# A new order of work for a spectral gate, with the stores spread over the last stage and a new place for some small products

## Chip, cores, metric

One core of a Trainium2 chip. The metric is the device time of one execution in microseconds. The profiled span is 1.8 us shorter than that time, but 2.1 to 2.2 us shorter in the three kernels that have the small products on VectorE (`b_small_dve`, `a_small_dve`, `b_both`), so about 0.4 us of what these seem to gain in a profile is lost outside the span; why is not shown. Where two profiles are compared, spans are used, where two kernels are compared, times. A run is called slow here when it is over 1.5% above the fastest of the same kernel. Comparisons use fast runs.

## The reference

```python
def branch(x, w_r, w_i):                       # x: 1 x 2048 x 1024, bf16
    X = rfft2(x.astype(float32), axes=(-2, -1))
    return irfft2(X * (w_r + 1j * w_i), s=(2048, 1024)).astype(bfloat16)

g = sigmoid((A_x * gate_w).sum(-1, keepdims=True))
return g * branch(A_x, A_w_r, A_w_i) + (1 - g) * branch(A_x, B_w_r, B_w_i)
```

Both branches share the input, so there is one forward transform, then two products with weights, two inverse transforms and a mix.

## The kernel before

The transforms are matmuls on TensorE. ScalarE and VectorE move the results out of PSUM, VectorE does folds, products and sums. The kernel is a list of named tasks. Each task names its engine and buffers, and each engine does its tasks in the order of the list; semaphores are derived from what the tasks read and write.

```python
SUMS = {(0, 3): 1, (0, 5): 1, (1, 6): 1}   # units (branch, j) summed on VectorE before the inverse transform
ORDER = """
mz:g x12:s F:s table:a warm:p0 x14:s x2:s x0:s x8:s x4:s w0.0.0.1:s fold6.0.2:d0 ...
... i1.15:p2 evv1.10:a p1.6.0:d2 i1.14:p1 evv1.15:a
gzg:d v5.1:p3 ps1.6.1:d evv1.14:a i1.11:p0 ...
... out10:s q12a:d s1i15:p00 y0b:d4 evo14.0:a out4:s evo14.1:a y12b:d1 out2:s q14a:d out0:s ...
"""
# name:engine+buffers; p TensorE, a ScalarE, d VectorE, g GpSimd, s the DMA queue
names = {"p": "pe", "a": "act", "d": "dve", "g": "pool", "s": "sp"}
```

The names that matter: `w1.*` load the second branch's weights; `p1.j.t` are its products and `ps1.j.t` their sums (VectorE); `i1.T` is the first inverse transform of row T (32 matmuls, or 16 if the unit is summed), `evv1.T` its eviction; `dinv`, `evd` the second inverse transform and its eviction; `s1i`, `evo` the mix of both branches; `q`, `h`, `y` the last sums, `out` a store of 512 or 256 KB. `p5.b` are the products of the single column l = 512, `v5.b` the 24 small matmuls that need them, `vf.b` the copy of that column into the row of all others:

```python
def e_p5(e_, b=b):           # four operations on 16 or 32 elements per partition
    x = ap(X5, 0, [[16, 2], [1, 16]]); r = ["X5"] + wk[b]        # X5 and all weights of the branch
    S.op("pool", [tt(ap(P5, o, ...), x, ap(T_, 512, ...), ALU.mult)], r, [("p5", b, 0)])
    S.op("pool", [tt(ap(P5, o + 32, ...), x, ap(T_, NS + 512, ...), ALU.mult)], r, [("p5", b, 1)])
    for c, op in enumerate((ALU.subtract, ALU.add)):
        S.op("pool", [tt(..., op)], [("p5", b, c)], [("P5", b, c)])
# the store of a group: one DMA, issued when both halves of its sums are there
S.op("sp", [lambda e: e.dma_start(outv[:, n:n + nn, :], yy(yb, 0, [[1, 1024]]))],
     [("y", yb.i, 0), ("y", yb.i, 1)], [], dma="out")
```

Of the kernel before, what the change touches and what calls it, by code (L numbers as in the profile page):

```python
# [13 lines left out]
SUMS = {(0, 3): 1, (0, 5): 1, (1, 6): 1}  # L14
# [7 lines left out]
mz:g x12:s F:s table:a warm:p0 x14:s x2:s x0:s x8:s x4:s w0.0.0.1:s fold6.0.2:d0 fold6.1.2:d1 fold6.0.1:d0  # L22
fold6.0.0:d0 fold6.1.1:d1 fold6.1.0:d1 neg2:a neg3:d DM:s fod6.1.1:d fod6.1.0:d fod6.0.1:d neg0:a fod6.0.0:d
w0.0.0.0:s s1.6.1:p1 neg1:a fold7.0.2:d0 fold7.0.1:d0 fold7.1.2:d1 fold7.1.0:d1 s1.6.0:p2 GW:s evz6.1:a fold7.1.1:d1
fold7.0.0:d0 SK:s fod7.1.1:d fod7.1.0:d s1.7.1:p3 fold1.0.0:d3 fold1.1.2:d2 fold1.0.1:d3 fold1.1.1:d2 evz6.0:a
fod7.0.0:d fod7.0.1:d w0.0.1.0:s fold1.1.0:d2 fold1.0.2:d3 s1.7.0:p0 fod1.1.0:d fod1.1.1:d evz7.1:a fold0.1.2:d2
fold0.0.0:d3 fold0.0.1:d3 fold0.0.2:d3 fold0.1.1:d2 fod0.0.0:d s1.1.1:p1 fod0.0.1:d evz7.0:a fod1.0.0:d fold0.1.0:d2
s1.0.0:p2 fod1.0.1:d fold4.0.0:d5 fold4.0.1:d5 fold4.1.2:d4 fod0.1.1:d fod0.1.0:d fold4.1.0:d4 s1.1.0:p3 evz0.0:a
fold4.1.1:d4 s1.0.1:p0 fold4.0.2:d5 fod4.1.0:d fod4.1.1:d evz1.1:a s1.5.1:p2 fold2.1.2:d1 fold2.0.1:d0 fold2.0.0:d0
# [341 lines left out]
def build(nc, A_x, A_w_r, A_w_i, B_w_r, B_w_i, gate_w, out):  # L371
# [53 lines left out]
    def tt(o, a, b, op):  # L425
        return lambda e: e.tensor_tensor(out=o, in0=a, in1=b, op=op)  # L426
# [673 lines left out]
```

## Time and profile before

| | before |
|---|---|
| time, median of 3 (range) | 125.28 us (125.12 to 125.44) |
| profiled span | 123.70 us |
| last sum over | 119.04 us |
| span behind the last sum | 4.66 us |
| TensorE's wait for the small products | 1.3 us |

How to read it: TensorE, VectorE and ScalarE are each busy for 86 to 91% of the span, so no engine can be called the bound; one has to ask, stage by stage, what the next stage waits for.

### The profile page before, as it was taken

The page shows a single profiled execution, that of the slowest core. Times are in us where ns is not written, and L with a number is a line of the kernel's source. Part 1 is how long each engine was busy: PE and PEld are TensorE (multiplying, and loading weights), DVE is VectorE, ACT ScalarE, POOL GpSimd, SP SyncE. Part 2 cuts the span into 40 slices and gives each one's busy share as a digit, 9 for nine tenths or more (in the row PEclk, how much of TensorE's full clock was granted, in tenths as well). Part 3 has the DMA queues.
Part 4 walks back from the last instruction along what each step waited for, and adds up shares of the span by engine and source line. Part 5 has one row for each costly group of instructions (what it writes and reads, how often), then busy time and mean ns, then how long its engine had stood idle before and what let it go on. Part 6 is the DMA issues. An engine that isn't in the chain of part 4 may idle for free.

```text
span 123.7 us, 4183 instructions
## 1 busy us (share of the span) xinstructions
PE 112.6 (91%) x1853; PEld 84.8 (69%) x1853; DVE 108.4 (88%) x155; ACT 105.8 (86%) x119; POOL 14.6 (12%) x22
## 2 busy tenths in 40 slices
PE   5999999999999999999999995999999999999700
PEld 2377888855768755886898895999967656476300
DVE  0589899699999999999999997699879989999940
ACT  4187799699999999997999999789988999999700
POOL 2000000220000069000000498000000000000000
PEclk9999999999999999999999999999999999999996
DMA  4999999677785878685027000000000000170897
GB/s 86 409 440 424 303 215 206 187 210 203 223 235 168 218 204 260 172 215 184 0 52 209 16 0 5 5 1 0 5 0 0 0 5 0 42 297 0 339 409 269
DMA packets 13425, 19.23 MB, mean 155 GB/s; under 512 B 2656, under 2 KB 10848, under 8 KB 13152
## 3 DMA queue, kind: packets, MB, share of 16 engines
q1 hardware_dynamic: 13408, 18.98, 49.0%
q8 instruction: 14, 0.23, 0.8%
q14 instruction: 3, 0.02, 0.1%
HBM read 14.77 MB, written 4.19 MB: 153 GB/s over the span
## 4 chain that ended last, share of the span: by engine, by line
PE 56%; ACT 25%; POOL 6%; SPq 3%; DMA 3%; issue 1%; DVE 1%; ACTq 0%; DVEq 0%; POOLq 0%
PE PS L423 56%; ACT R L430 17%; ACT RING L430 8%; POOL P L426 6%; SPq L446 3%; DMA R<-in_B_w_i_dram 3%; POOL R L516 0%; ACTq L287 0%; DVE RING L426 0%; DVEq L287 0%; DVE R L426 0%; POOLq L287 0%; ACT X L430 0%; POOLq L1085 0%
## 5 line engine op out<-in xcount | busy, mean ns | idle before, releaser
L430 ACT ACTIVATE R<-PS 128x1024 bf16<-128x1024 f32 (+1 forms) x97 | 90.1, 1079 | 6.6 <-PE PS L423 6.4
L426 DVE TENSOR_TENSOR RING<-R 128x2048 bf16<-128x2048 bf16 (+2 forms) x69 | 58.1, 897 | 5.4 <-DMA R<-in_A_x_dram 5.3
L423 PE MATMUL PS<-DM,R 128*128 128x128 bf16 (+1 forms) x384 | 34.2, 246 | 0.0
L423 PEld LDWEIGHTS PS<-DM,R 128*128 128x128 bf16 x384 | 28.8, 98 | 4.8 <-ACT R L430 0.4
L423 PE MATMUL PS<-SK,RING 64*128 64x128 bf16 x928 | 28.9, 217 | 1.0 <-ACT R L430 0.8
L423 PEld LDWEIGHTS PS<-SK,RING 64*128 64x128 bf16 x928 | 26.5, 103 | 4.3 <-ACT R L430 2.6
L431 DVE CAST R<-PS 128x1024 bf16<-128x1024 f32 x17 | 20.4, 1221 | 3.1 <-PE PS L423 3.0
L423 PE MATMUL PS<-R,FM 128*128 128x512 bf16 (+1 forms) x80 | 17.7, 358 | 0.0
L426 DVE TENSOR_TENSOR R<-R 128x512 bf16<-128x512 bf16 (+2 forms) x30 | 13.8, 512 | 0.5 <-ACT R L430 0.3
L426 POOL TENSOR_TENSOR P<-X,R 128x32 bf16<-128x32 bf16 x4 | 9.2, 2330 | 38.7 <-DMA R<-in_B_w_i_dram 20.2
L423 PEld LDWEIGHTS PS<-R,FM 128*128 128x128 bf16 x80 | 7.4, 98 | 6.8 <-ACT R L430 1.3
L430 ACT ACTIVATE RING<-PS 128x1024 bf16<-128x1024 f32 x11 | 10.7, 1060 | 0.5 <-PE PS L423 0.5
L423 PE MATMUL PS<-FM,RING 128*128 128x256 bf16 (+1 forms) x74 | 9.3, 281 | 0.0
L423 PE MATMUL PS<-RING,SK 64*64 64x512 bf16 (+1 forms) x128 | 8.9, 384 | 0.3 <-ACT R L430 0.2
L423 PEld LDWEIGHTS PS<-FM,RING 128*128 128x128 bf16 x74 | 7.2, 98 | 1.9 <-DVE RING L426 0.2
L423 PE MATMUL PS<-R 128*128 128x512 bf16 x16 | 5.8, 542 | 1.3 <-POOL R L516 1.3
L423 PE MATMUL PS<-FM,R 128*128 128x256 bf16 x56 | 6.8, 273 | 0.0
L431 DVE CAST RING<-PS 128x1024 bf16<-128x1024 f32 x5 | 6.1, 1223 | 0.3 <-PE PS L423 0.2
L423 PEld LDWEIGHTS PS<-FM,R 128*128 128x128 bf16 x56 | 5.4, 98 | 0.9 <-DVE R L426 0.3
L423 PEld LDWEIGHTS PS<-RING,SK 64*64 64x64 bf16 x128 | 2.7, 105 | 4.6 <-ACT RING L430 1.7
L423 PEld LDWEIGHTS PS<-R 128*128 128x128 bf16 x16 | 2.0, 133 | 4.5 <-issue 2.7
L426 DVE TENSOR_TENSOR R<-RING 128x512 bf16<-128x512 bf16 (+1 forms) x10 | 4.8, 527 | 0.0
(38 smaller groups left out, 36.3 us busy)
## 6 DMA issues: line engine op xcount, KB each, us to landing
out_dram<-RING SPq DMA_DIRECT2D x7, 512.0 KB, 3.6
R<-in_A_x_dram SPq DMA_DIRECT2D x4, 512.0 KB, 5.9
R<-in_A_x_dram SPq DMA_DIRECT2D x2, 1024.0 KB, 10.2
R<-in_A_w_r_dram SPq DMA_DIRECT2D x15, 128.2 KB, 3.1
R<-in_A_w_i_dram SPq DMA_DIRECT2D x15, 128.2 KB, 3.0
R<-in_B_w_r_dram SPq DMA_DIRECT2D x15, 128.2 KB, 3.0
R<-in_B_w_i_dram SPq DMA_DIRECT2D x15, 128.2 KB, 3.1
FM<-c_F SPq DMA_DIRECT2D x1, 512.0 KB, 4.6
```

The lines of the kernel that those rows point to most:

```text
L423: return lambda e: e.matmul(o, l, r, start=start, stop=stop, skip_group_check=True)
L426: return lambda e: e.tensor_tensor(out=o, in0=a, in1=b, op=op)
L430: return lambda e: e.activation(o, i, ACT.Copy)
L431: return lambda e: e.tensor_copy(o, i)
L446: t.emit = lambda g: S.op(eng, [lambda e, d=d, s=s: e.dma_start(d, s, **kw) for d, s in pairs], reads, writes, dma=kind, after=after)
```

## The change

Its words: a new order of work, the stores spread over the last stage, and the small products of l = 512 of the second branch on VectorE. The diff, without most of the list of tasks:

```diff
-SUMS = {(0, 3): 1, (0, 5): 1, (1, 6): 1}
+SUMS = {(0, 1): 1, (0, 4): 1, (1, 3): 1, (1, 7): 1}
 ORDER = """
-mz:g x12:s F:s ... w1.4.1.0:s ... RM:s ... w1.8.1.1:s w1.12.0.0:s ... w1.12.0.1:s ... GS:s ... w1.12.1.0:s
+mz:g x2:s F:s ... w1.12.0.0:s ... grow:p0 RM:s ... w1.8.1.1:s ... vf0:s ... w1.12.0.1:s ... w1.12.1.0:s
-... ps1.4.0:d p5.1:g i1.7:p3 ... i1.14:p1 evv1.15:a gzg:d v5.1:p3 ps1.6.1:d ...
+... dinv0.9:p2 evd0.8:a p5.1:g dinv0.3:p3 ps1.3.0:d ... i1.13:p1 ps1.7.0:d v5.1:p3 ...
-... out6 ... out8 ... out10 ... out4 ... out2 ... out0 ... out12 ... out14 ... out15
+... out2 ... out4 ... out10 ... out8 ... out6 ... out0 ... out12 ... out15 ... out14
 """
-        p5 = add(f"p5.{b}", due("v", 1 + b), {"pool": (5.0, 5.2)}, None, ...)
+        p5 = add(f"p5.{b}", due("v", 1 + b), {"pool": (7.5, 7.7), "dve": (0.6, 0.7)}, None, ...)
-            S.op("pool", [tt(ap(P5, o, ...
+            S.op(e_, [tt(ap(P5, o, ...            # likewise in the other three operations
+        o.bytes, o.tail = nn * 262144 / 410e3, 0.3   # estimates for the ordering, not used on the chip
```

More of the change, by code (lines that the diff above doesn't have):

```diff
@@ L21 @@
 ORDER = """
-mz:g x12:s F:s table:a warm:p0 x14:s x2:s x0:s x8:s x4:s w0.0.0.1:s fold6.0.2:d0 fold6.1.2:d1 fold6.0.1:d0
-fold6.0.0:d0 fold6.1.1:d1 fold6.1.0:d1 neg2:a neg3:d DM:s fod6.1.1:d fod6.1.0:d fod6.0.1:d neg0:a fod6.0.0:d
-w0.0.0.0:s s1.6.1:p1 neg1:a fold7.0.2:d0 fold7.0.1:d0 fold7.1.2:d1 fold7.1.0:d1 s1.6.0:p2 GW:s evz6.1:a fold7.1.1:d1
-fold7.0.0:d0 SK:s fod7.1.1:d fod7.1.0:d s1.7.1:p3 fold1.0.0:d3 fold1.1.2:d2 fold1.0.1:d3 fold1.1.1:d2 evz6.0:a
-fod7.0.0:d fod7.0.1:d w0.0.1.0:s fold1.1.0:d2 fold1.0.2:d3 s1.7.0:p0 fod1.1.0:d fod1.1.1:d evz7.1:a fold0.1.2:d2
@@ L27 @@
-fold0.0.0:d3 fold0.0.1:d3 fold0.0.2:d3 fold0.1.1:d2 fod0.0.0:d s1.1.1:p1 fod0.0.1:d evz7.0:a fod1.0.0:d fold0.1.0:d2
-s1.0.0:p2 fod1.0.1:d fold4.0.0:d5 fold4.0.1:d5 fold4.1.2:d4 fod0.1.1:d fod0.1.0:d fold4.1.0:d4 s1.1.0:p3 evz0.0:a
-fold4.1.1:d4 s1.0.1:p0 fold4.0.2:d5 fod4.1.0:d fod4.1.1:d evz1.1:a s1.5.1:p2 fold2.1.2:d1 fold2.0.1:d0 fold2.0.0:d0
-fold2.1.1:d1 evz0.1:a s1.4.1:p1 fold2.1.0:d1 evz1.0:a fod4.0.1:d fod2.1.1:d fod2.1.0:d s1.2.1:p0 fod4.0.0:d evz5.1:a
-s1.3.1:p3 fold2.0.2:d0 evz4.1:a s1.5.0:p2 evz3.1:a w0.0.1.1:s fod2.0.0:d s1.4.0:p1 fod2.0.1:d evz2.1:a s1.2.0:p3
@@ L32 @@
-evz4.0:d w0.4.0.0:s evz5.0:a s1.3.0:p0 evz2.0:d d0.1:p10 evz3.0:a d2.1:p21 d3.1:p31 d3.0:p31 gj:p0 d2.0:p21 evq3:a
-g8:d d0.0:p10 evq2:d g9:g d10.1:p02 w0.4.0.1:s d10.0:p02 evq0:a d11.0:p32 d11.1:p32 qc1:d d1.0:p20 evq10:a evq11:d
-d1.1:p20 w0.4.1.0:s s2.1.1:p1 evq1:a s2.1.0:p0 evx1.1:d s2.5.0:p3 w0.4.1.1:s evx1.0:a s2.0.0:p2 qc0:d qc5:d s2.0.1:p1
-evx0.0:d evx5.0:a w0.8.0.0:s d14.0:p01 d14.1:p01 evx0.1:a p0.1.0:d0 s2.5.1:p3 d15.0:p21 w0.8.0.1:s evx5.1:a d15.1:p21
-evq14:d d5.1:p10 ps0.1.0:d evq15:a d5.0:p10 d4.1:p30 w0.8.1.0:s p0.1.1:d0 d6.0:p02 evq5:a d4.0:p30 d6.1:p02 d7.1:p22
@@ L37 @@
-qc7:d evq4:a w0.8.1.1:s evq6:d ps0.1.1:d d7.0:p22 s2.7.1:p1 evq7:a s2.2.0:p3 qc2:d evx7.1:d w0.12.0.0:s s2.7.0:p0
-evx2.0:a s2.2.1:p2 p0.0.1:d1 d9.0:p11 evx2.1:a d9.1:p11 w0.12.0.1:s i0.3:p3 p0.0.0:d1 evq9:a ps0.0.1:d i0.2:p2
-w0.12.1.0:s evx7.0:a evv0.3:d ps0.0.0:d d8.1:p11 evv0.2:a w0.12.1.1:s d8.0:p11 p0.5.1:d0 d12.0:p00 d13.1:p30 evq8:a
-d13.0:p30 d12.1:p00 p0.5.0:d0 w1.0.0.0:s evq13:a s2.4.0:p2 s2.4.1:p1 evq12:d evx4.0:a i0.0:p3 w1.0.0.1:s evx4.1:a
-qc3:d ps0.5.0:d i0.1:p2 qc6:d evv0.0:a qc4:d ps0.5.1:d w1.0.1.0:s x5:p0 s2.6.0:p1 p0.2.1:d1 x5e:a evv0.1:a s2.6.1:p3
@@ L42 @@
-p5.0:g w1.0.1.1:s i0.11:p0 p0.2.0:d1 evx6.0:a ps0.2.1:d i0.10:p2 evv0.11:a p0.4.0:d0 w1.4.0.0:s ps0.2.0:d i0.4:p1
-evx6.1:a i0.5:p0 p0.4.1:d0 ps0.4.0:d w1.4.0.1:s evv0.4:a s2.3.0:p3 p0.6.1:d1 ps0.4.1:d evv0.5:a s2.3.1:p1 w1.4.1.0:s
-p0.6.0:d1 evx3.1:a ps0.6.1:d i0.9:p0 RM:s evx3.0:a p0.7.1:d2 i0.8:p1 ps0.6.0:d evv0.10:a i0.13:p3 p0.7.0:d2 w1.8.0.0:s
-ps0.7.1:d evv0.9:a v5.0:p2 p0.3.0:d0 ps0.7.0:d v5e.0:a w1.8.0.1:s i0.14:p0 evv0.13:a p0.3.1:d0 i0.12:p2 w1.4.1.1:s
-evv0.14:a ps0.3.0:d grow:p3 evv0.8:a p1.0.1:d1 w1.8.1.1:s evv0.12:a ps0.3.1:d i0.15:p0 ps1.0.1:d p1.0.0:d1 w1.12.0.0:s
@@ L47 @@
-i0.7:p1 evv0.15:a p1.1.0:d2 ps1.0.0:d i1.1:p2 w1.8.1.0:s evv0.7:a i0.6:p0 p1.1.1:d2 ps1.1.0:d DI:s i1.0:p1 evv0.6:a
-p1.2.1:d0 ps1.1.1:d evv1.0:a vf0:s i1.3:p0 w1.12.1.1:s p1.2.0:d0 evv1.1:a ps1.2.1:d i1.2:p1 evv1.3:a p1.3.0:d1
-w1.12.0.1:s ps1.2.0:d i1.4:p2 evv1.2:a gzr:d GS:s ps1.3.0:d i1.5:p0 w1.12.1.0:s evv1.4:a p1.4.1:d2 dinv0.3:p1 evv1.5:a
-p1.3.1:d1 dinv0.7:p3 ps1.4.1:d evd0.3:a dinv0.11:p2 p1.4.0:d2 ps1.3.1:d dinv0.9:p0 evd0.7:a i1.6:p1 p1.5.1:d0 evd0.9:a
-ps1.4.0:d p5.1:g i1.7:p3 evd0.11:a p1.5.0:d0 ps1.5.1:d gzt:p0 evv1.6:a p1.7.0:d1 i1.9:p2 ps1.5.0:d evv1.7:a i1.8:p1
@@ L52 @@
-p1.7.1:d1 ps1.7.0:d evv1.9:a i1.10:p3 p1.6.1:d2 evv1.8:a ps1.7.1:d i1.15:p2 evv1.10:a p1.6.0:d2 i1.14:p1 evv1.15:a
-gzg:d v5.1:p3 ps1.6.1:d evv1.14:a i1.11:p0 ps1.6.0:d v5e.1:a i1.13:p2 evv1.11:d i1.12:p1 evv1.13:a gmix1:p3 evv1.12:d
-dinv0.8:p0 sig1:a dinv0.0:p2 evd0.8:d vf1:s gmix0:p1 evd0.0:a dinv0.2:p3 ra1:d dinv0.1:p0 sig0:a evd0.2:d dinv0.4:p2
-evd0.1:a dinv0.13:p1 ra0:d dinv0.6:p3 rb1:d evd0.13:a evd0.4:d dinv0.10:p0 evd0.6:a dinv0.5:p1 rb0:d dinv1.5:p2
-evd0.10:a nr0:d dinv1.2:p3 evd0.5:d nr1:a dinv1.11:p0 evd1.5:a evd1.2:d dinv1.3:p1 evd1.11:a dinv1.7:p2 evd1.3:a
@@ L57 @@
-dinv1.6:p3 evd1.7:d dinv1.4:p0 evd1.6:a s1i2:p10 evd1.4:d s1i3:p20 evo2.0:a dinv1.1:p3 evo3.0:d dinv1.8:p0 evd1.1:a
-dinv1.9:p1 q2a:d evd1.8:a q2b:d s1i7:p21 h2a:d0 evd1.9:a s1i6:p31 h2b:d0 evo7.0:a dinv1.10:p0 y2b:d0 dinv1.0:p1 y2a:d0
-evo6.0:a evd1.10:d s1i9:p22 evd1.0:a s1i8:p32 q6a:d evo9.0:a q6b:d s1i5:p03 h6b:d1 evo8.0:a h6a:d1 s1i4:p13 evo5.0:a
-q8a:d dinv1.12:p2 q8b:d y6a:d1 evo4.0:a s1i0:p30 h8b:d0 evd1.12:a s1i1:p00 q4b:d h8a:d0 evo0.0:a dinv0.12:p1 q4a:d
-y8b:d2 dinv1.13:p2 evo1.0:a y8a:d2 dinv1.15:p3 evd0.12:a h4b:d0 s1i11:p01 q0b:d evd1.13:a y6b:d1 s1i10:p11 q0a:d
@@ L62 @@
-evo11.0:a out6:s s1i12:p22 h4a:d0 out8:s h0b:d1 evo10.0:a y4b:d3 evd1.15:a dinv1.14:p0 y4a:d3 dinv0.14:p1 q10b:d
-evo12.0:a q10a:d s1i13:p32 h0a:d1 evd0.14:a h10b:d0 h10a:d0 evd1.14:a dinv0.15:p2 y0a:d4 evo13.0:a s1i14:p13 y10a:d5
-y10b:d5 evd0.15:a q12b:d out10:s q12a:d s1i15:p00 y0b:d4 evo14.0:a out4:s evo14.1:a y12b:d1 out2:s q14a:d out0:s
-q14b:d y12a:d1 evo15.1:a y14b:d2 evo15.0:a out12:s y14a:d2 q15a:d out14:s q15b:d y15b:d5 y15a:d5 out15:s
+mz:g x2:s F:s table:a warm:p0 x14:s x0:s x12:s x4:s x8:s w0.0.1.0:s fold1.1.2:d1 fold1.0.2:d0 fold1.0.0:d0
@@ new lines @@
+fold1.0.1:d0 fold1.1.0:d1 SK:s fold1.1.1:d1 GS:s neg2:a neg0:d fod1.1.1:d fod1.1.0:d fod1.0.0:d neg3:a DM:s fod1.0.1:d
+s1.1.1:p1 neg1:a w0.0.0.0:s fold7.0.2:d3 fold7.1.1:d2 fold7.1.2:d2 s1.1.0:p2 fold7.0.1:d3 evz1.1:a fold7.0.0:d3
+w0.0.0.1:s fold7.1.0:d2 fod7.0.0:d fod7.0.1:d s1.7.0:p3 fold0.0.1:d0 fold0.1.2:d1 fold0.0.0:d0 evz1.0:a fold0.0.2:d0
+fod7.1.0:d fod7.1.1:d fold0.1.1:d1 fold0.1.0:d1 GW:s fold6.1.2:d2 fold6.0.0:d3 fold6.0.1:d3 fold6.0.2:d3 fod0.1.1:d
+fod0.1.0:d s1.7.1:p0 fod0.0.1:d fod0.0.0:d fold6.1.1:d2 evz7.1:a s1.0.0:p1 fold6.1.0:d2 fod6.0.1:d fod6.1.1:d
@@ new lines @@
+fod6.1.0:d s1.6.1:p2 fod6.0.0:d evz7.0:a fold2.0.1:d5 fold2.0.0:d5 fold2.1.2:d4 fold2.1.0:d4 s1.6.0:p0 fold2.1.1:d4
+evz6.1:a fold2.0.2:d5 fod2.1.0:d fod2.1.1:d s1.2.1:p3 evz6.0:a s1.0.1:p2 evz0.0:a fold4.1.0:d0 fold4.1.2:d0
+fold4.0.1:d3 fold4.0.0:d3 s1.3.1:p0 fold4.1.1:d0 evz0.1:a fod2.0.0:d fod4.1.0:d fod4.1.1:d s1.5.1:p1 evz2.1:a
+fod2.0.1:d s1.4.1:p2 fold4.0.2:d3 evz5.1:a s1.2.0:p3 evz3.1:a fod4.0.1:d s1.3.0:p1 fod4.0.0:d evz4.1:a w0.0.1.1:s
+evz2.0:d s1.5.0:p0 evz3.0:a s1.4.0:p2 evz5.0:d w0.4.0.0:s d0.1:p30 evz4.0:a d3.1:p11 w0.4.0.1:s d1.1:p00 d1.0:p00
@@ new lines @@
+d0.0:p30 evq1:a d2.1:p21 evq0:d d2.0:p21 d3.0:p11 evq2:a d6.0:p02 d6.1:p02 evq3:d qc0:a s2.0.1:p3 evq6:a w0.4.1.0:s
+s2.0.0:p2 evx0.1:d s2.1.1:p1 qc1:a evx0.0:a s2.1.0:p0 w0.4.1.1:s evx1.1:d d7.1:p32 evx1.0:a d7.0:p32 d11.1:p20
+p0.0.1:d0 evq7:a d11.0:p20 w0.8.0.0:s d10.1:p10 d10.0:p10 evq11:a p0.0.0:d0 s2.3.0:p0 ps0.0.1:d w0.8.0.1:s s2.3.1:p3
+evx3.0:a d5.0:p21 qc3:d evq10:d ps0.0.0:d d5.1:p21 evx3.1:a d12.0:p02 w0.8.1.0:s d12.1:p02 p0.1.1:d1 d4.1:p11 evq5:a
+d4.0:p11 s2.5.0:p3 w0.8.1.1:s evq12:d evq4:a d13.1:p22 d13.0:p22 evx5.0:a qc5:d s2.5.1:p1 qc2:d evq13:d w0.12.0.0:s
@@ new lines @@
+s2.2.1:p0 evx5.1:a s2.2.0:p3 evx2.1:d s2.6.0:p2 w0.12.0.1:s evx2.0:a d15.1:p10 p0.1.0:d1 evx6.0:a d8.1:p01 gj:p3
+w0.12.1.0:s d15.0:p10 d8.0:p01 g8:a evq15:a ps0.1.1:d d14.0:p20 g9:g d14.1:p20 ps0.1.0:d d9.0:p31 evq8:a w0.12.1.1:s
+d9.1:p31 evq14:d s2.6.1:p1 evq9:a i0.2:p0 w1.0.0.0:s qc6:d evx6.1:d i0.3:p2 evv0.2:a i0.0:p3 p0.3.0:d1 evv0.3:a
+w1.0.0.1:s i0.1:p1 evv0.0:a qc7:d qc4:d s2.7.1:p0 p0.3.1:d1 ps0.3.0:d x5:p2 w1.0.1.0:s evv0.1:a s2.4.0:p3 p0.5.1:d0
+ps0.3.1:d x5e:a evx7.1:a s2.4.1:p1 w1.0.1.1:s s2.7.0:p2 p0.5.0:d0 ps0.5.1:d evx4.0:a i0.7:p0 w1.4.0.0:s evx4.1:a
@@ new lines @@
+p0.2.0:d2 ps0.5.0:d i0.11:p3 evx7.0:a p5.0:g i0.6:p1 p0.2.1:d2 ps0.2.0:d evv0.11:a i0.10:p2 p0.6.0:d1 ps0.2.1:d
+evv0.7:a w1.4.1.0:s i0.4:p3 p0.6.1:d1 evv0.6:a ps0.6.0:d i0.5:p0 w1.4.0.1:s evv0.4:a p0.4.1:d0 ps0.6.1:d i0.12:p1
+w1.4.1.1:s i0.13:p3 p0.7.0:d2 evv0.12:a evv0.10:a p0.7.1:d2 ps0.7.0:d w1.8.0.1:s evv0.5:a p0.4.0:d0 ps0.7.1:d i0.14:p1
+w1.8.0.0:s evv0.13:a i0.15:p2 ps0.4.1:d evv0.14:a DI:s ps0.4.0:d w1.8.1.0:s p1.0.1:d1 i0.8:p0 i0.9:p3 evv0.8:a
+w1.12.0.0:s v5.0:p1 p1.0.0:d1 ps1.0.1:d evv0.15:a grow:p0 RM:s p1.2.1:d2 ps1.0.0:d evv0.9:a w1.8.1.1:s p1.1.0:d0
@@ new lines @@
+v5e.0:a ps1.2.1:d i1.0:p2 vf0:s p1.1.1:d0 i1.1:p3 ps1.1.0:d evv1.0:a gzr:d evv1.1:a ps1.1.1:d i1.2:p1 w1.12.1.1:s
+p1.2.0:d2 i1.3:p2 evv1.2:a w1.12.0.1:s p1.3.0:d1 ps1.2.0:d i1.5:p0 evv1.3:a i1.4:p3 p1.3.1:d1 evv1.5:a w1.12.1.0:s
+dinv0.12:p1 evv1.4:a p1.5.0:d0 dinv0.0:p2 evd0.12:a ps1.3.1:d dinv0.6:p0 ps1.5.0:d p1.4.0:d2 evd0.0:a gzt:p3
+dinv0.8:p1 evd0.6:a gzg:d p1.4.1:d2 ps1.4.0:d dinv0.9:p2 evd0.8:a p5.1:g dinv0.3:p3 ps1.3.0:d ps1.4.1:d evd0.9:a
+gmix0:p0 evd0.3:d i1.7:p1 sig0:a i1.6:p2 p1.5.1:d0 dinv0.10:p3 evv1.7:a i1.9:p0 p1.6.1:d1 ps1.5.1:d evv1.6:a i1.8:p1
@@ new lines @@
+evv1.9:a p1.6.0:d1 ps1.6.1:d i1.11:p2 evv1.8:a p1.7.0:d2 ps1.6.0:d i1.12:p0 evd0.10:a p1.7.1:d2 i1.13:p1 evv1.12:a
+ps1.7.0:d v5.1:p3 evv1.11:a i1.10:p0 ps1.7.1:d v5e.1:a evv1.13:d i1.15:p2 evv1.10:a i1.14:p3 evv1.15:d dinv0.11:p1
+evv1.14:a gmix1:p0 evd0.11:d dinv0.4:p2 vf1:s sig1:a dinv0.5:p3 ra0:d evd0.4:a dinv0.2:p1 rb0:d dinv0.7:p0 evd0.5:a
+evd0.2:d dinv0.13:p2 evd0.7:a dinv1.2:p3 ra1:d dinv1.6:p1 evd0.13:d evd1.2:a dinv1.3:p0 rb1:d dinv1.8:p3 evd1.3:a
+evd1.6:d s1i2:p20 evd1.8:a dinv1.10:p0 evo2.0:d nr0:a dinv1.12:p1 evd1.10:a s1i3:p30 evd1.12:d dinv1.4:p2 evo3.0:a
@@ new lines @@
+nr1:d dinv1.5:p0 evd1.4:a q2a:d dinv1.9:p1 evd1.5:d dinv1.13:p3 evd1.9:a dinv1.11:p2 q2b:d evd1.13:a h2a:d0 s1i9:p01
+h2b:d0 evd1.11:a dinv1.7:p1 y2a:d0 s1i8:p31 evo9.0:a evd1.7:d s1i4:p22 evo8.0:a y2b:d0 s1i5:p02 evo4.0:a q8a:d out2:s
+q8b:d dinv1.0:p1 evo5.0:a h8b:d1 s1i10:p33 h8a:d1 evd1.0:a s1i11:p23 q4b:d q4a:d evo10.0:a y8a:d1 s1i6:p00 y8b:d1
+evo11.0:a s1i7:p10 h4b:d0 evo6.0:a dinv0.1:p3 q10b:d h4a:d0 dinv1.1:p2 evo7.0:a q10a:d y4b:d2 dinv1.15:p0 evd1.1:a
+h10a:d1 s1i13:p11 evd0.1:a q6a:d y4a:d2 evd1.15:a q6b:d out4:s s1i1:p22 h10b:d1 evo13.0:a h6a:d0 s1i0:p32 h6b:d0
@@ L66 @@
+evo1.0:a dinv0.15:p0 y10a:d3 evo0.0:a dinv0.14:p1 y6b:d4 s1i12:p21 y10b:d3 evd0.14:a q0a:d out10:s q0b:d evd0.15:a
+y6a:d4 out8:s dinv1.14:p3 h0a:d1 out6:s evo12.0:a s1i15:p13 h0b:d1 evd1.14:a q12b:d q12a:d y0b:d5 s1i14:p00 evo15.1:a
+y0a:d5 evo15.0:a y12a:d0 out0:s q15a:d q15b:d y12b:d0 evo14.1:a evo14.0:a y15b:d2 out12:s y15a:d2 q14b:d out15:s
+q14a:d y14b:d3 y14a:d3 out14:s
 """
@@ L321, in __init__ @@
         self.bytes = self.ni = 0
+        self.tail = 1.6
         self.alt, self.skip, self.state, self.soft = None, False, 0, []
@@ L457, in xload @@
         t = load(f"x{a}", [(ap(R1, a * 1024, [[1024, b - a], [1, 1024]]), xv[:, a:b, :])],
-                 [("x", i // 2) for i in range(a, b, 2)], (b - a) * 262144, 425.0)
+                 [("x", i // 2) for i in range(a, b, 2)], (b - a) * 262144, 400.0)
         for i in range(a, b, 2):
@@ L831, in build @@
     for b in range(2):
-        p5 = add(f"p5.{b}", due("v", 1 + b), {"pool": (5.0, 5.2)}, None, [t_x5e] + [w for j in range(8) for w in tW[b, j]])
+        p5 = add(f"p5.{b}", due("v", 1 + b), {"pool": (7.5, 7.7), "dve": (0.6, 0.7)}, None, [t_x5e] + [w for j in range(8) for w in tW[b, j]])
         def e_p5(e_, b=b):
@@ L837, in e_p5 @@
             r = ["X5"] + wk[b]
-            S.op("pool", [tt(ap(P5, o, [[16, 2], [1, 16]]), x, ap(T_, 512, [[NS, 2], [2 * NS, 16]]), ALU.mult)], r, [("p5", b, 0)])
-            S.op("pool", [tt(ap(P5, o + 32, [[16, 2], [1, 16]]), x, ap(T_, NS + 512, [[-NS, 2], [2 * NS, 16]]), ALU.mult)], r, [("p5", b, 1)])
+            S.op(e_, [tt(ap(P5, o, [[16, 2], [1, 16]]), x, ap(T_, 512, [[NS, 2], [2 * NS, 16]]), ALU.mult)], r, [("p5", b, 0)])
+            S.op(e_, [tt(ap(P5, o + 32, [[16, 2], [1, 16]]), x, ap(T_, NS + 512, [[-NS, 2], [2 * NS, 16]]), ALU.mult)], r, [("p5", b, 1)])
             for c, op in enumerate((ALU.subtract, ALU.add)):
-                S.op("pool", [tt(ap(P5, o + 64 + 16 * c, [[1, 16]]), ap(P5, o + 32 * c, [[1, 16]]), ap(P5, o + 32 * c + 16, [[1, 16]]), op)],
+                S.op(e_, [tt(ap(P5, o + 64 + 16 * c, [[1, 16]]), ap(P5, o + 32 * c, [[1, 16]]), ap(P5, o + 32 * c + 16, [[1, 16]]), op)],
                      [("p5", b, c)], [("P5", b, c)])
```

## The prediction

> **What bounds the kernel now.** I read the page first, then the chain of waits, then the waits themselves, then the two stretches that these point to. The page says that nobody is idle enough to name one engine:
>
> ```profile
> PE 112.6 (91%) x1853; PEld 84.8 (69%) x1853; DVE 108.4 (88%) x155; ACT 105.8 (86%) x119; POOL 14.6 (12%) x22
> ```
>
> So the time goes by stage. The chain that ended last says which (start, length, what):
>
> ```profile
> 44.17 9.18 ACT R L430 x10
> ...
> 66.29 3.37 DMA R<-in_B_w_i_dram
> 69.72 6.89 POOL P L426 x3
> 76.61 0.18 POOLq L287
> 76.80 0.14 issue
> 76.93 39.68 PE PS L423 x423
> 116.61 0.02 issue
> 116.63 0.60 ACT R L430
> ```
>
> Up to about 54 us ScalarE's evictions carry it. Then the last weight load of the second branch ends at 69.65, and GpSimd takes until 76.79 for the four small products of l = 512. TensorE needs them for its 24 tiny matmuls (the task v5.1), which stand in front of others in its queue. From 76.93 it runs 39.7 us without a real gap, then come two half evictions, the last sums and the stores.
>
> The price of the GpSimd stretch is a line in the table of waits, and on VectorE an idle spell before the casts at 78.53 (timeline):
>
> ```profile
> PE PS L423 <- POOL P L426: 1.3, 1, 1.3
> ```
>
> and
>
> ```profile
> 78.53 3.49 DVE L431 CAST R<-PS 128x1024 bf16<-128x1024 f32 x3 [2.00 <-PE PS L423]
> ```
>
> Why are four operations on 16 to 32 elements 7 us long? GpSimd's and VectorE's timelines side by side:
>
> ```profile
> 69.72 5.59 POOL L426 TENSOR_TENSOR P<-X,R 128x32 bf16<-128x32 bf16 x1 [20.19 <-DMA R<-in_B_w_i_dram]
> ```
>
> ```profile
> 68.29 6.89 DVE L426 TENSOR_TENSOR RING<-R 128x2048 bf16<-128x2048 bf16 x6
> 75.10 0.17 DVE L426 TENSOR_TENSOR ZG<-PS,GS 128x16 bf16<-128x16 f32 x1
> 75.19 1.35 DVE L426 TENSOR_TENSOR RING<-RING 128x1024 bf16<-128x1024 bf16 x2
> ```
>
> The first small product ended at 75.31, just behind VectorE's unbroken row of large products (to 75.18). [...]
>
> The end of the kernel, by microsecond (PE, PEld, DVE, ACT, POOL busy, then the clock, the DMA share and GB/s):
>
> ```profile
> 110.00:111.00 1.00, 1.00 (x11) 0.78 (x9) 1.00 (x4) 1.00 (x3) 0.00 (x0) 1.00 0.52 201
> 111.00:112.00 1.00, 1.00 (x9) 0.64 (x7) 1.00 (x3) 1.00 (x2) 0.00 (x0) 1.00 0.00 0
> 113.00:114.00 1.00, 1.00 (x8) 0.64 (x7) 1.00 (x3) 1.00 (x2) 0.00 (x0) 1.00 0.00 0
> 115.00:116.00 1.00, 1.00 (x9) 0.69 (x8) 1.00 (x3) 0.89 (x2) 0.00 (x0) 1.00 1.00 401
> 119.00:120.00 1.00, 0.00 (x0) 0.00 (x0) 0.04 (x1) 0.00 (x0) 0.00 (x0) 1.00 1.00 397
> 122.00:123.00 1.00, 0.00 (x0) 0.00 (x0) 0.00 (x0) 0.00 (x0) 0.00 (x0) 0.50 0.77 291
> ```
>
> The stores do nothing from 110.5 to 114, then run at about 400 GB/s until 122.8, while the last sum is over at 119.04. The order of the stores explains it: out6, out8, out10, out4, out2, out0, out12, out14, out15 in one queue. The pair of sums for out2 was ready at 97.5 and that for out4 at 109.8, but both stand behind out10, whose sums end at 114.05. From there seven stores are left, five of 512 KB and two of 256 KB, 3.07 MB. That at 401 GB/s is 7.7 us; the queue cannot be empty before 114.9 + 7.7 = 122.6, whatever the engines do. The end is bound by the backlog of stores.
>
> [...] In the first branch the four operations, beside the same sort of row from 44.2 us on, took 1.2 to 1.8 us each[...]. [...] The trace gives 401 GB/s when packed; out10 was issued at 114.08, its bytes began at about 114.9 (0.8 us), and from the last byte (122.8) to the end of the span are 0.9 us. [...]
>
> **The change, part by part.** I compared the two lists of tasks: the same 542, in another order.
>
> Stores. The new order is out2, out4, out10, out8, out6, out0, out12, out15, out14. Counting back from the end E of the last sum with VectorE's steps (0.33 to 0.4 us for a sum of 512 columns, 0.61 for one of 1024, 0.25 for 256), the stores can go at about E-14 (out4), E-9.3 (out10), E-8.9, E-7.2, E-3.9 (out0), E-2.5, E-1.3 and E; out2 long before. Each half megabyte takes 1.3 us, so at E only a remnant of out15 is under way. The last store then ends at E + 0.8 (to first byte) + 0.65 (256 KB at 401 GB/s) + 0.9 (completion) = E + 2.4. Now it is 123.70 - 119.04 = E + 4.66. Gain 2.3; I take 2.1, some of the stores being later than counted.
>
> Small products. The words say VectorE, but the new list has "p5.1:g", and the letter g still means GpSimd; the assignment function is untouched. What changes is the table of costs (7.5 us for GpSimd in place of 5), a possible emission on VectorE that this list does not choose, and the place of v5.1. In the new list seven inverse products (dinv; four before), ten unhalved and two halved transforms and two gate groups lie between the last weight loads and v5.1. Worked out from the trace: after the first full copy of the small row (vf0, at 61.31 now) the last load lands 8.3 us later, without the gate table in between about 7.7, and GpSimd needs 7: ready 14.7 us after vf0. TensorE's work from there to v5.1 is ten transforms of 0.93 us, two halved ones, seven dinv of 0.65 (8 instructions at 82 ns) and two gate groups of 0.6: 16.0 us. So the 1.35 us should vanish, with a small margin. [...] I give it 0.6 of 1.35: 0.8 us gained.
>
> Sums on VectorE. Four units of two rows are summed before their transform, now three: two transforms fall from 32 to 16 matmuls, 2 x 0.45 = 0.9 us less TensorE; two sums of 0.6 us more VectorE. Evictions and copies moved between engines: VectorE one cast of 1.14 more, two tiny copies (0.17 each) and one of the gate (0.17) fewer; ScalarE the reverse. VectorE is loaded by 1.2 + 0.6 = 1.8 us before about 77 us, where it has had nearly no gap since 24 us; but its 2.0 us of idleness at 76.5 is in the same stretch. Net of both engines I put 0.3 us lost.
>
> Head: the loads are renamed and permuted, with the same sizes (512 KB first, then the transform table), so zero. The other, shorter waits of the order (ScalarE 0.71, 0.35, 0.23, 0.46, VectorE 0.46, 0.50 after 78 us): a new list may mend some or make others; 0.3 us gained.
>
> Sum: 2.1 + 0.8 - 0.3 + 0.3 = 2.9 us, 125.28 to **122.4 us**.
>
> **Rivals.** (a) The small products stay a wait[...], with v5.1 standing in front of i1.10, i1.15 and i1.14. For it: the assignment is unchanged. [...] Then 0.8 us of the gain goes and perhaps 0.5 more: 123.2 to 123.7. (b) VectorE becomes the bound before 77 us: +1.8 us on an engine that is full from 24 to 76 us, TensorE waiting for products. For it: 14.54 of 15 us busy between 62 and 77. Against: three more dinv tasks give TensorE something to do meanwhile. Time 123 to 123.8. (c) The second branch's small row (vf1) reaches its place later than TensorE comes to dinv1.2: there are six dinv and a gate group (4.5 us) after the last transform, now nine and two (7 us); eviction 1.3 plus issue and landing 2.2 make 3.5, so it should hold; else 0.5 us. (d) All comes off: 1.35, half the sum, the stores: 121.
>
> **Range and chances.** The gain at the stores is nearly sure (1.6 to 2.3), because it is queue order and bytes. By itself it is 1.7%, short of 2% (122.77 us). The other terms decide, from 1.5 us better to 1 worse, so somewhat more than half for faster; slower would take a loss of 4.6 us elsewhere. Range 120.9 to 124.1.
>
> **What would show it.** Right: no stretch of zero GB/s between stores followed by 8 us at 400; the last store issued within 0.1 us of the last sum and landing about 2.4 us later; no wait of TensorE on GpSimd's P. Wrong: TensorE or VectorE idle for over 1 us around v5.1; TensorE waiting for RING of VectorE between 50 and 77 us; the last matmul later than 116.6.

Cuts in it are marked: they took out statements on the hardware that no trace of this case shows, and no term of the sum. It stands as 2.1 + 0.8 - 0.3 + 0.3 = 2.9 us, from 125.28 to 122.4. The 0.6 in the second term (0.6 of 1.35 us) was the guess of a chance. The 0.8 and 0.9 us around the last store's bytes are measured on the kernel before: out10 was issued at 114.08 and its first byte moved at 114.91; the last byte of all stores moved at 122.88, the last store's landing is recorded at 123.23, and the span ends at 123.70. So what the sum calls completion is the whole stretch from the last byte to the end of the span.

## The result, and the profile after

All outputs were correct. Four executions took 124.32, 122.16, 122.26 and 124.36 us; those of the kernel before on the same chip 125.12 to 125.52. The two of 122.2 count as fast. The ratio of the fast runs is 0.975 (95% interval 0.972 to 0.978), so 2.5% faster. That leaves out the slow half; by the medians of all four runs on each side (123.29 against 125.36) the gain is 2.07 us or 1.7%. Ratios here are the mean time of one kernel's fast runs over the mean of the other's fast runs of the same rounds, so not quite the ratio of the medians.

The profile that came with this result was of the first run, a slow one, although its granted clock of 0.992 was not lower than in the fast runs (0.995 and 0.987). So the changed kernel was run again, as `a_same`, and that profile (122.14 us, fast) is the one to lay beside the profile of before. The six runs were spread evenly from 122.14 to 123.76 us.

| span, us | before | after, fast (`a_same`) | after, slow |
|---|---|---|---|
| last sum over | 119.04 | 117.74 | 119.91 |
| span behind the last sum | 4.66 | 2.61 | 2.61 |
| span | 123.70 | 120.35 | 122.53 |

The last sum before, and after in the fast execution (timeline of VectorE; start plus length is the time in the table):

```profile
118.28 0.76 DVE L426 TENSOR_TENSOR RING<-R 128x512 bf16<-128x512 bf16 x2
116.98 0.76 DVE L428 TENSOR_TENSOR RING<-R 128x512 bf16<-128x512 bf16 x2
```

The end of the fast execution, by microsecond (busy time of PE, PEld, DVE, ACT, POOL, then the clock, the DMA share and GB/s):

```profile
107.00:108.00 1.00, 1.00 (x9) 0.61 (x8) 1.00 (x3) 1.00 (x2) 0.00 (x0) 1.00 0.87 352
111.00:112.00 1.00, 1.00 (x10) 0.65 (x9) 1.00 (x2) 1.00 (x3) 0.00 (x0) 1.00 1.05 418
114.00:115.00 1.00, 1.00 (x9) 0.59 (x6) 1.00 (x4) 0.44 (x1) 0.00 (x0) 1.00 0.40 152
116.00:117.00 1.00, 0.00 (x0) 0.00 (x0) 0.96 (x5) 0.27 (x1) 0.00 (x0) 1.00 0.69 274
118.00:119.00 1.00, 0.00 (x0) 0.00 (x0) 0.00 (x0) 0.00 (x0) 0.00 (x0) 0.94 1.01 375
119.00:120.00 1.00, 0.00 (x0) 0.00 (x0) 0.00 (x0) 0.00 (x0) 0.00 (x0) 0.50 0.41 154
```

The stores now begin early and the queue drains between them (152 and 274 GB/s), so the last one finds little ahead of it: at the last sum 0.36 MB of earlier stores are still to be moved. It lands 2.1 us after its issue, where before the last one took 3.75 us. What follows the last sum is now mostly one store's own time.

The small products in the same execution (timeline of GpSimd):

```profile
69.83 1.74 POOL L428 TENSOR_TENSOR P<-X,R 128x32 bf16<-128x32 bf16 x2 [17.60 <-DMA R<-in_B_w_i_dram]
71.53 0.39 POOL L428 TENSOR_TENSOR P<-P 128x16 bf16<-128x16 bf16 x2
```

They are still on GpSimd, and ready at 71.9 us; TensorE takes them at 78.0, without the wait it had before (timelines, before and after):

```profile
76.93 0.54 PE L423 MATMUL PS<-P,SK 64*16 64x1 bf16 x24 [1.35 <-POOL P L426]
77.99 0.56 PE L425 MATMUL PS<-P,SK 64*16 64x1 bf16 x24
```

In the table of waits no line of TensorE names them any more, but a new one is there:

```profile
PE PS L425 <- DVE RING L428: 1.7, 2, 1.4
```

and the chain that ended last runs along VectorE (its casts and products, start and length) to 62.5 us, where before it ran along ScalarE and TensorE:

```profile
46.24 9.41 DVE RING L428 x9
...
56.11 6.37 DVE RING L428 x6
62.53 9.53 PE PS L425 x264
72.06 20.78 PE PS L425 x405
92.87 11.55 ACT R L432 x13
```

The slow execution differs from this one in a single stretch of 8 us. Its weight loads on TensorE (timeline):

```profile
60.17 1.80 PEld L425 LDWEIGHTS PS<-SK,RING 64*128 64x128 bf16 x64 [0.42 <-ACT R L432]
63.37 3.62 PEld L425 LDWEIGHTS PS<-SK,RING 64*128 64x128 bf16 x128 [1.39 <-issue]
68.33 1.66 PEld L425 LDWEIGHTS PS<-DM,R 128*128 128x128 bf16 x21 [1.34 <-ACT R L432]
```

Twice TensorE stood still for over a microsecond, once with "issue" as the reason, which means that it waited for nothing that the profile shows. In the fast execution the same place reads:

```profile
60.45 1.80 PEld L425 LDWEIGHTS PS<-SK,RING 64*128 64x128 bf16 x64 [0.42 <-ACT R L432]
62.52 3.60 PEld L425 LDWEIGHTS PS<-SK,RING 64*128 64x128 bf16 x128 [0.27 <-DVE RING L428]
66.23 1.88 PEld L425 LDWEIGHTS PS<-DM,R 128*128 128x128 bf16 x24
```

I subtracted the start of each TensorE instruction in one execution from that of the same instruction in the other. The difference is about -0.3 us from 17 us on (the input arrived a little earlier in the slow one), jumps by 1.4 us at instruction 1985 and by 1.2 us at instruction 2241 (counted over TensorE's recorded instructions), and is 2.2 us at the end. 2241 - 1985 is 256. The page has a line for a DMA queue that no task uses:

```profile
q8 instruction: 14, 0.23, 0.8%
```

14 packets of 16 KB; the trace does not say for which engine. TensorE has 3,678 recorded instructions in the slow execution, every other engine at most 180, and 3,678 in pieces of 256 would be 14.4. So my estimate from these numbers is that the packets hold TensorE's instructions, 256 in each; with the seventh and the eighth put to 1985 and 2241, the first is the one before instruction 449. Counted so, the first 13 packets of the slow execution begin 181 to 267 instructions ahead of their place, but for two: those before 1985 and 2241 begin 110 and 90 ahead, and of these 13 places they are the only ones with a pause of TensorE over 0.25 us (1.35 and 1.28). That TensorE pauses because its instructions are not there yet would fit, but no record says so.

### The profile page after: what moved, and what is told of

Read it like the earlier page. It is cut to its first block, busy times and chain, and to the rows that moved or that the text cites. A ratio compares the mean times of both kernels' runs of the same rounds, so it can differ in the third digit from the quotient of the medians.

```text
span 122.5 us, 4126 instructions
## 1 busy us (share of the span) xinstructions
PE 111.1 (91%) x1821; PEld 84.0 (69%) x1821; DVE 110.1 (90%) x155; ACT 105.3 (86%) x121; POOL 12.7 (10%) x22
## 4 chain that ended last, share of the span: by engine, by line
PE 34%; DVE 29%; ACT 18%; DMA 9%; issue 4%; SPq 2%; DVEq 1%
PE PS L425 34%; DVE RING L428 20%; ACT R L432 18%; DMA R<-in_A_x_dram 9%; DVE RING L433 5%; DVE R L433 3%; SPq L448 2%; DVE R L428 1%; DVE QC L433 0%; DVEq L288 0%; DVEq L274 0%
## 5 line engine op out<-in xcount | busy, mean ns | idle before, releaser
L425 PE MATMUL PS<-DM,R 128*128 128x256 bf16 (+1 forms) x384 | 35.2, 246 | 0.0
L425 PE MATMUL PS<-SK,RING 64*128 64x128 bf16 x896 | 27.6, 217 | 4.1 <-DVE RING L428 1.7
L425 PEld LDWEIGHTS PS<-SK,RING 64*128 64x128 bf16 x896 | 25.5, 103 | 5.5 <-DVE RING L428 2.1
L432 ACT ACTIVATE RING<-PS 128x1024 bf16<-128x1024 f32 x10 | 9.8, 1055 | 0.5 <-PE PS L425 0.5
L428 POOL TENSOR_TENSOR P<-X,R 128x32 bf16<-128x32 bf16 x4 | 6.8, 1720 | 20.3 <-DMA R<-in_B_w_i_dram 16.5
L433 DVE CAST RING<-PS 128x1024 bf16<-128x1024 f32 x6 | 7.2, 1220 | 1.4 <-PE PS L425 1.4
L425 PE MATMUL PS<-R 128*128 128x512 bf16 x16 | 5.3, 501 | 1.3 <-POOL R L518 1.3
L428 POOL TENSOR_TENSOR GW<-GW 128x8 bf16<-128x8 bf16 (+1 forms) x4 | 1.7, 445 | 36.7 <-ACT GW L432 36.7
L428 DVE TENSOR_TENSOR RING<-RING 128x1024 bf16<-128x1024 bf16 x8 | 5.2, 684 | 0.0
```

Of the source, the lines that this page charges most:

```text
L425: return lambda e: e.matmul(o, l, r, start=start, stop=stop, skip_group_check=True)
L428: return lambda e: e.tensor_tensor(out=o, in0=a, in1=b, op=op)
L432: return lambda e: e.activation(o, i, ACT.Copy)
L433: return lambda e: e.tensor_copy(o, i)
```

## The experiments

Four questions: is the end really the stores; what is the wait for the small products worth, and does the engine matter; are the added sums good or bad; and what are the pauses. Shared runs of the kernel before on one chip are the denominator of the ratios.

### The stores alone: `b_stores`

The kernel before, with only the nine stores moved in the list, each behind its own last sum:

```diff
-... out6:s ... out8:s ... out10:s ... out4:s ... out2:s ... out0:s ... out12:s ... out14:s ... out15:s
+... y2a:d0 out2:s ... y8a:d2 out8:s ... y6b:d1 out6:s ... y4a:d3 out4:s ... y10b:d5 out10:s ... y0b:d4 out0:s ... y12a:d1 out12:s ... out14:s ... out15:s
```

> The kernel before with nothing changed but the order of the stores in the queue (each one right behind its own sums). Theory (the end is a backlog of stores): the last sum stays at 119.0 us, the span ends 2.4 to 2.9 us behind it in place of 4.66, so 1.75 to 2.25 us less: 123.0 to 123.6 us. Rival (the engines set the end, the stores are hidden): under 0.5 us less.

Measured: 123.23 to 123.88 us, ratio 0.983 (0.981 to 0.986), mean 123.62 against 125.75, so 2.1 us less. In the profile the last sum is over at 119.28 (not earlier than before), and the span ends 2.51 us behind it. The theory holds, the rival falls. The last store, of 256 KB, landed 2.0 us after its issue; at 401 GB/s its bytes take 0.65 us, which leaves an estimated 1.35 us beside the bytes. The first one, of 512 KB with nothing ahead of it, landed after 2.65 us, which gives the same. The same table of the end as above:

```profile
113.00:114.00 1.00, 1.00 (x10) 0.63 (x8) 1.00 (x3) 1.00 (x3) 0.00 (x0) 1.00 0.00 0
120.00:121.00 1.00, 0.00 (x0) 0.00 (x0) 0.00 (x0) 0.00 (x0) 0.00 (x0) 0.50 0.82 305
121.00:121.80 0.80, 0.00 (x0) 0.00 (x0) 0.00 (x0) 0.00 (x0) 0.00 (x0) 0.50 0.00 0
```

At 113 us the queue is still idle, as before, but now because it has nothing left over: out2, out8, out6 and out4 are gone.

### The small products alone: `b_small_dve`

The kernel before with `p5.1:d` in place of `p5.1:g`, its operations emitted on the task's own engine, moved to just behind `p1.6.1`:

```diff
-... p1.5.1:d0 evd0.9:a ps1.4.0:d p5.1:g ...
+... p1.6.1:d2 p5.1:d ...
```

> The kernel before with the four small products of l = 512 of the second branch on VectorE, placed behind the products of its unit 6. Theory (TensorE's 1.35 us wait for them delays all that follows): 1.0 to 1.4 us less, the end being kept back in part by the stores, so 0.7 to 1.4. Rival (VectorE and ScalarE had work in that time, and set the pace): under 0.4 us less, and other waits of TensorE just behind.

Measured: 124.69 to 126.2 us, ratio 0.997 (0.993 to 1.001). The profiled run: last sum at 118.13, so 0.91 us earlier than before, span 122.79, again 4.66 behind the last sum. On VectorE the four operations are short (timeline):

```profile
74.45 0.33 DVE L426 TENSOR_TENSOR P<-X,R 128x32 bf16<-128x32 bf16 x2
74.71 0.28 DVE L426 TENSOR_TENSOR P<-P 128x16 bf16<-128x16 bf16 x2
```

TensorE's gap from 75.6 to 76.9 us is gone. The profiled span says 0.9 us, but the same two executions differ by only 0.5 us in time (125.49 and 124.96), since 2.2 us in place of 1.8 lie outside the span. The four times say 0.4 us and leave room for nothing at all, so the expected 0.7 to 1.4 us did not come. Taken alone this is inconclusive; the last experiment below settles it better.

### The changed kernel with the small products really on VectorE: `a_small_dve`

```diff
-... dinv0.9:p2 evd0.8:a p5.1:g dinv0.3:p3 ...
+... dinv0.9:p2 evd0.8:a p5.1:d dinv0.3:p3 ...
```

> The changed kernel with the small products of the second branch really on VectorE, as the words of the change say, at the same place of the list. In the fast profile GpSimd has them ready at 71.9 us and TensorE takes them at 78.0. Theory (the wait is gone through the place, not the engine): the same within 0.3 us, with VectorE 0.5 us more busy. Rival (GpSimd still costs something[...]): 0.4 us or more less.

Measured: four fast runs of 122.70 to 124.18, two slow ones (124.8, 124.9), ratio of the fast ones 0.985; not better, and by the ratio worse than the unchanged one (0.979). The profiled run (123.7 us) has pauses of 0.29 us at instruction 1985 and 1.00 us at 2241; TensorE runs 1.1 us behind the fast unchanged kernel behind these two, and hardly loses more up to 87 us. So the products on VectorE bring nothing, since there was no wait left to take away. The times lie outside the expected 0.3 us: by the ratios they are about 0.75 us longer, of which 0.35 us is the part outside the span; whether the rest is pauses alone, these runs don't settle.

### The sums of one unit taken away: `a_unsum04`, `a_unsum17`

```diff
-SUMS = {(0, 1): 1, (0, 4): 1, (1, 3): 1, (1, 7): 1}
+SUMS = {(0, 1): 1, (1, 3): 1, (1, 7): 1}      # a_unsum04
+SUMS = {(0, 1): 1, (0, 4): 1, (1, 3): 1}      # a_unsum17
```

> The changed kernel without the sums of unit 4 of the first branch: two VectorE sums of 0.6 us less, two transforms of 32 matmuls in place of 16, 0.9 us more of TensorE. The fast profile's chain is VectorE up to 62.5 us, and TensorE waits 1.38 and 0.36 us for VectorE at 54.5 and 56.9. Theory (VectorE is the bound up to there, as the prediction's second rival said): 0.4 to 1.0 us less than the unchanged changed kernel on the same chip. Rival (TensorE is the bound): 0.5 to 0.9 us more.

> The changed kernel without the sums of unit 7 of the second branch, at 78 us, where the chain is TensorE. Theory (here TensorE is the bound, so the sums pay): 0.4 to 0.9 us more. Rival (VectorE is the bound everywhere): 0.4 us or more less.

Measured: `a_unsum04` 122.03 to 123.37, ratio 0.978, where the unchanged kernel has 0.979 and 0.978 on two other chips: no difference. Both the theory and the rival miss. Of TensorE's two waits for VectorE the longer stays (1.38 us, up to 54.0), the shorter goes, and the 32 more matmuls fill its room; up to 66 us TensorE keeps the distance to `a_same` that it had at 50 us (0.5 us ahead). The chain along TensorE now begins at 54 us, not at 62.5. At this place the two engines are in balance. After it this profile has a pause of 0.67 us, at instruction 2497. `a_unsum17`: three fast runs, ratio 0.984, three slow ones; its profiled run of 124.75 us has pauses of 1.42 and 0.73 us. Its span of 122.96 less these is 120.8, against 120.35: an estimate of 0.5 us lost by giving up the sums there, in line with the theory, but drawn from one profile and a kernel with many slow runs.

### The pauses: `a_same`, `a_rm_late`, `a_rm_early`, and both again

The slow profile has its DMA engines full from 56 to 60.7 us (DMA share 0.95 to 1.14 by the microsecond), with the second branch's weights and, among them, the 512 KB load of the gate matrix (RM), which the kernel before issues 11 us earlier. (The fast profile has them nearly full for as long, to 61.0 us, so this alone does not set the two apart.) Does moving this one load take the pauses away? The edits:

```diff
-... w1.12.0.0:s ... grow:p0 RM:s ... w1.8.1.1:s ...
+... w1.12.1.0:s RM:s ...                      # a_rm_late
+... w1.4.1.0:s RM:s ...                       # a_rm_early, as before
```

> The changed kernel again, to get a profile of a fast execution and more times. Theory[...]: the runs fall again into two groups near 122.2 and 124.3 us, and a fast profile has no pause of 1.2 to 1.4 us between two instructions of TensorE at its instructions 1985 and 2241, or at most one of them; the slow one has both. Rival (a state of the chip, such as the clock): the kernel before, run on the same chip, is in two groups too, or the slow runs are longer everywhere.

> The changed kernel with the 512 KB load of the gate matrix moved from amid the second branch's weights to behind the last of them. Theory (this load fills the DMA engines at 56 to 60.7 us of the slow profile[...]): the slow group disappears or becomes rare, and all runs are at 122.3 us or below. Rival (the two groups have another cause): slow runs are as frequent as in the unchanged kernel, about half.

> The changed kernel with the 512 KB load of the gate matrix where the kernel before has it, among the first weights of the second branch (45 to 50 us). Theory[...]: no pause of TensorE at its instructions 1985 or 2241 in the profile, times with less spread than the unchanged changed kernel (1.6 us) and a median 0.3 to 0.9 us lower. Rival: same spread and median, pauses at the same or another multiple of 256 instructions.

> The changed kernel once more, only so that the next run stands beside it on the same chip: 122.1 to 124.4 us, median near 123.

> The changed kernel with the load of the gate matrix among the first weights of the second branch, again. Theory[...]: mean 0.4 to 0.9 us below the unchanged changed kernel of the same call, no run of the slow group. Rival (the earlier difference was the chip's): within 0.2 us of it.

| kernel | runs, us | mean of the fast | ratio |
|---|---|---|---|
| `a_same` | 122.14 to 123.76 | 123.04 | 0.979 |
| `a_rm_late` | 122.33 to 123.80 | 123.09 | 0.979 |
| `a_rm_early` (another chip) | 121.54 to 122.93 | 122.21 | 0.975 |
| `a_same2` | 122.05 to 123.63 | 122.84 | 0.978 |
| `a_rm_early2` | 121.71 to 122.65 | 122.21 | 0.973 |

Two groups did not come back: on these chips the times fill the range between 122.1 and 123.8 us, so the expectation for `a_same` was right only in its fast profile. The intervals of the ratios of `a_same` and `a_same2` reach to 0.983 and 0.985, so that the gain is over 2% is not sure on these chips. `a_rm_late` failed: no better than unchanged. Its profile has smaller pauses at both places (0.31 and 0.46 us). With the load early the times are lower: in the one call that has both, 0.6 us by the means, about twice the standard error of that difference, and a spread of 0.9 in place of 1.6 us.

What goes with the pauses can be read from all profiles together. For the two packets of q8 that by the estimate above belong to TensorE's instructions 1985 and 2241 (the seventh and the eighth; worked out from the trace's single records): how many instructions TensorE still had before that place when the packet began, and how long it paused at that place.

```text
profiled run      time     1985: left, pause    2241: left, pause
a_same           122.14      193   0.00           255   0.05
a_dummy          121.94      164   0.01           205   0.05
a_rm_early       121.54      173   0.01           229   0.05
a_rm_early2      122.25      172   0.00           213   0.05
a_unsum04        122.03      142   0.00           161   0.23
a_rm_late        122.90      148   0.31           141   0.46
a_same2          123.32       94   1.12           125   0.45
a_small_dve      123.70      132   0.29            99   1.00
after (slow)     124.32      110   1.35            90   1.28
a_unsum17        124.75      109   1.42           149   0.73
before           125.49      170   0.03           189   0.03
```

In this table, with 160 or more instructions left there is at most 0.23 us of pause, with under 130 always one of 0.4 to 1.4 us, and between them from none to 0.7. In all these runs TensorE goes on no sooner than 1.25 us after the packet's bytes have been moved (1.92 and 1.37 us in `before`, 1.57 and 1.42 in `after`). The sum of the two pauses goes, roughly, with the time of the run (0.05 us at 122.14, 2.63 at 124.32). So these pauses are what "slow" means in the two slow runs of these kernels that were profiled (`after` and `a_unsum17`), and it is not their clock (0.992 and 0.999). It need not hold for every slow run: on another chip, four of eleven runs of the kernel before were slow too (127.2 to 127.83 us, clock 0.976 to 0.989), and none of them was profiled. Nor is a pause always a loss: the profile of `a_rm_early2` has two others, 1.20 us at instruction 1473 and 0.86 us at 1729, and runs at 122.25 us. They fall at 52 and 57 us, where VectorE is the bound; TensorE is back within 0.2 us of `a_same` at 62.5 us.

### More load on the DMA engines at that time: `a_dummy`

```diff
+    DUM = sb("DUM", 256)
+    load("dum", [(ap(DUM, 0, [[32, 8], [1, 32]]), AP(cst["RM"], 0, [[2048, 128], [256, 8], [1, 32]]))], ["DUM"], ...)
-... grow:p0 RM:s p1.2.1:d2 ...
+... grow:p0 RM:s dum:s p1.2.1:d2 ...
```

> The changed kernel with one more load behind that of the gate matrix: 64 KB in 1024 pieces of 64 bytes, never read, which keeps the DMA engines busy for an estimated 3 us more (1024 pieces, at 0.05 us each as the weights' pieces took, over 16 engines)[...]. Theory[...]: nearly every run in the slow group, near 124.3 us or above, with a pause of TensorE of 1.2 us or more at instruction 1985 in the profile, while VectorE does not wait for weights. Rival (another cause): times as the unchanged kernel's, or longer by a wait of VectorE for weights.

Measured: 121.94, 122.26 and 122.64 us, and one slow run of 125.99. The expectation fails. In the profile the DMA engines are full until 59.4 us (DMA share 0.93 to 1.25 by the microsecond from 55 to 59), as wanted, and yet the packet before instruction 1985 begins at 58.9 with 164 instructions left, and the pause is 0.01 us. The estimate of 3 us rested on the weights' pieces, which are of 1026 bytes and took 47 ns (median, 40 to 62 us of `before` and `after`); how long the 64-byte ones took is not in the record. But the test was weaker than meant: in this execution the gate matrix was issued at 53.4 us, against 56.0 in the slow and 57.0 in the fast unchanged one, so even with the added load the engines were full for no longer than there (to 60.7 and 61.0). Since the fast profile too has them busy until 61.0, and its packet begins with 193 instructions left, full engines did not by themselves come with a late packet here. What decides when a packet of q8 begins is left open. Which DMA engine moves it, and what that engine is doing at that moment, would be the next thing to look at, but no run here shows it.

### The two parts in the old order: `b_both`

The kernel before with both edits, of `b_stores` and of `b_small_dve`, and nothing else.

> The kernel before with its stores in the order of their sums and with the small products of the second branch on VectorE: the two parts together, in the old order of work. By the single runs 1.7% and 0.3%, in the profiles 2.15 and 0.9 us. Theory (they add up, since one is at the end and the other on TensorE's path): 122.7 to 123.4 us, so that the rest of the new order is worth little. Rival (the new order itself carries the gain): no better than the stores alone, 123.7.

Measured: 122.40 to 122.63 us, just below the expected 122.7 to 123.4; ratio 0.976 (0.970 to 0.982). The changed kernel (`a_same2`) has 0.978, with a spread of 1.6 us in place of 0.2. The profile: last sum at 117.93, span 120.45, so 2.52 us behind it, and no wait of TensorE for the small products:

```profile
75.68 0.56 PE L423 MATMUL PS<-P,SK 64*16 64x1 bf16 x24
```

Against `b_stores` (0.983, another chip, the two intervals just touching) that is 0.7% or 0.9 us of time for the small products; in the profiles the last sum comes 1.35 us earlier, of which 0.4 is lost outside the span. The two parts add up, and the old order with them is as fast as the new one on average; only the changed kernel's undisturbed executions (122.05 to 122.26) are some 0.4 us shorter.

No version here is clearly best: `a_rm_early` (122.21, twice) and `b_both` (122.54, nearly without spread) are both a little below the changed kernel in the means, and the intervals of their ratios overlap.

## Why the prediction was right

Predicted were 122.4 us in a range of 120.9 to 124.1; the fast runs are at 122.2, all runs at a median of 123.29. For the undisturbed executions the working holds term by term, as follows. That the median of all runs stays in the range is luck: half of the runs were 2 us longer, the longest (124.36) outside the range, for a reason that no term allowed for. By its steps:

- **Stores.** Said: E + 2.4 in place of E + 4.66, 2.1 us gained. Found: E + 2.61 in the changed kernel, E + 2.51 with the stores alone, 2.05 and 2.1 us. The step was right in kind and size, and it is the greater part of the gain. In its working, 3.07 MB counts a KB as a thousand bytes; seven stores are 3.15 MB, 7.8 us at 401 GB/s, which fits the trace as well (last byte at 122.9). The stores went later than counted, as it had allowed: out4 at E - 12.0 in place of E - 14, out10 at E - 8.1 in place of E - 9.3.
- **Small products.** Said: still on GpSimd in spite of the change's words; the wait probably gone; 0.8 us as 0.6 of 1.35. Found: on GpSimd, wait gone; in the old order, where moving the products to VectorE took it away, it was worth 0.9 us (`b_both` against `b_stores`), and that it is worth as much in the new order is argued from that. The margin was not 1.3 us, as the working had it, but 6 us (ready at 71.9, taken at 78.0), because GpSimd needed 2.1 us and not 7: its first product took 1.52 us and ended at 71.35, just after a short row on VectorE (to 71.23), and VectorE's next long row (5.75 us) came only at 72.28. In the kernel before the first product of this branch took 5.59 us beside a row of products of 1.22 us each, and ended 0.13 us behind that row, while the four operations of the first branch took 1.2 to 1.8 us; in `a_same` one of the first branch took 4.04 us. What decides between these is not shown. Rival (a) fell.
- **Sums and VectorE's load.** Said: 0.3 us lost net, and as rival (b) that VectorE might become the bound. Found: it did, up to 62.5 us, with waits of TensorE of 1.4 and 0.4 us, one of the signs that I had put down as "wrong". It cost little: taking one unit's sums away changed nothing. The sign was too sharp; TensorE has slack there, since it does not set the end of that stretch.
- **Other waits of the new list.** Said: 0.3 us gained. Found in an undisturbed execution: the last sum is at 117.74, in `b_both` at 117.93, so 0.2 us for all the rest of the new order, the sums with it. That is one profile each, where single runs of one kernel differ by more; the two terms of 0.3 us were not measured apart. Rival (c) did not come: behind 62.5 us no wait of TensorE is listed in `a_same`.
- **Sum.** In the profiles 123.70 - 120.35 = 3.35 us, of which 2.05 are the stores, about 1.1 the wait (119.04 - 117.93 in `b_both`), 0.2 the rest. I had 2.9: 0.3 us too little for the wait and 0.2 for the rest.

What I did not see at all are the pauses. The one profile of the kernel before did not point to them: at the same two places its packets began with 170 and 189 instructions left, and its pauses were 0.03 us. In the new order an execution takes up to 2.2 us more, with the pauses at these two places. Why the new order is prone to them is not shown. Its rows of short matmuls are no denser than those before (192 in 5.85 us, against 256 in 8.24 us there); one difference is that the burst of loads lasts to about 61 us (DMA share 1.14 from 60 to 60.7 in the slow profile, 0.35 after that) in place of 58 (0.97 from 57 to 58 before, then 0.14). Through the pauses, the last matmul of the slow execution ended at 117.3, later than the 116.6 that I had put down as a sign of "wrong".

## What to carry to other kernels

Put each store where its data is ready, not where it was thought of: here the stores were issued in the order of the list, and out2, with its sums ready at 97.5 us, went at 114.93, behind out10 at 114.08. Look at the last stretch for zero GB/s ahead of full bandwidth (here no store's bytes from 110.68 to 114.91 us, then about 400 GB/s). Read the code of a change and not its title: here the engine never changed, and the wait went because other work was put in front of it. And where times of one kernel spread at an unchanged clock (here 122.16 to 124.36 us at 0.987 to 0.997), subtract two executions instruction by instruction: the place where the difference jumps says more than any average.
